# A new order of work in the engines' queues, from unit 12 of the third block to the end

## The chip, the cores and the metric

One core of one Trainium2 chip runs the whole kernel. The metric is device time in microseconds of that core, lower is better. The engines are TensorE (PE), VectorE (DVE), ScalarE (ACT), GpSimd (POOL) and SyncE (SP); each works off its own queue in the order of the program text, and DMAs are issued by SP and by ACT.

## The reference

Three layers follow each other on 1536 tokens of width 512, all in float32.

```python
# 1: attention with decay, 2 x 8 heads, 768 steps of 64, in blocks of 64
out[:, :, sl] = ((qb @ kb.T) * Dmask) @ vb + (qb * lam_pow) @ kv_state
# 2: x @ w_in (512 x 2048), leaky relu, @ w_out (2048 x 512)
g = np.maximum(0.01 * h, h)
# 3: h = x @ w_in (512 x 1024)
solu = h * softmax(h)
ln = (solu - mean(solu)) / np.sqrt(var(solu) + 1e-06) * g_ln
out = ln @ w_out            # 1024 x 512
```

## The kernel before

Every float32 matrix is split into a high and a low piece, and each product is three groups of matmuls: high by high, high by low, low by high. The pieces of an activation are made by a copy on ACT (high) and a subtraction on DVE (low).

Layer 2 runs in three blocks of 512 tokens; a block has 16 units, one for each 128 columns of the hidden layer. Unit f computes L1 (`l1_mm`, 12 matmuls into one of two `hps` banks), ACT and DVE turn the bank into a high and a low piece (`l1_split`: Prelu, copy, subtraction), and L2 of the unit before (`l2_mm`, 12 matmuls) adds to the four `acc` banks. After unit 15 the four banks are split into `xhi` and `xlo`, the input of layer 3 (`l2_split`, lines 458 to 461).

Layer 3 runs over six pairs of token tiles of 128 rows, two pairs to a block. A pair's h (two tiles by 1024) comes from seven products of six matmuls (`product`, Strassen's scheme in Winograd's form), each into a bank, and `h2_sum` adds the bank into the tiles. Product 1 is copied out of its bank by ACT (line 609); the others are added by DVE, four of them with a running maximum. In pairs 1 to 5 products 1 and 2 share bank `aps[0]`, 6 and 3 `aps[1]`, 5 and 4 `hps[0]`. The sums of x that five of the products need are made by POOL (`sums_x`) and split by ACT and DVE (`pieces_x`, lines 545 and 547).

Each of the twelve tiles t is then normed: `norm_max` (DVE), `norm_exp` (ACT), `norm_mul` (DVE: multiply, scale, and a transpose inside 32 x 32 blocks, line 646), `norm_square` (ACT, then two small POOL operations that give the row factor). `ln_turn` moves the blocks with 16 DMAs of 32 KB into a tile `lt`, so that the tile is turned; n of the 16 are issued by ACT, the rest by SP (line 663). `ln_pieces` splits the turned tile (ACT line 685, DVE line 687). `out_mm` does 24 matmuls into bank `acc[2]` or `acc[3]` (line 703), ACT evicts with the row factor (line 706), SP stores. Tiles 9 and 11 are turned by TensorE (`ln_transpose`, line 670).

The order of the text is the order of each queue; nothing reorders it. Pair 0 lies in the units 12 to 15 of the third block, two products after the L2 of units 12, 13 and 14 (`turn0`) and the last in unit 15. Both of its tiles are normed and turned in unit 15, ACT issuing 6 and 8 of the DMAs. Then come, in this order, `l2_split`, pair 1 with tile 0's pieces, output tiles 0 and 2, pair 2, and so on (lines 1027 to 1054). `h2(p, late, between, early)` puts a tile's pieces at one of three places of a pair; ACT issues 4 of the 16 DMAs of each later tile, right behind its `norm_square`.

Of the kernel before, what the change touches and what calls it, by code (L numbers as in the profile page):

```python
# [16 lines left out]
P = 128  # L17
# [12 lines left out]
FF2 = 1024  # L30
# [14 lines left out]
def fused_kernel(ctx: ExitStack, tc: tile.TileContext, att, vt, tab, cst, w_in, w_out, w_in2, w_out2, out):  # L45
# [590 lines left out]
    def norm_mul(t):  # L636

        e, h = wide(t, 0), wide(t, 1)
        dve.scalar_tensor_tensor(e, h, 1.0, e, op0=ALU.mult, op1=ALU.mult, accum_out=col(t, SU))  # L639
        dst, src = h, e  # L640
        if t not in ON_PE:
            src = e.rearrange("p (k j c) -> p j k c", j=GRP, c=32)
            dst = h.rearrange("p (j k c) -> p j k c", j=GRP, c=32)
        dve.tensor_scalar(dst, src, float(FF2), col(t, SU), op0=ALU.mult, op1=ALU.subtract)  # L644
        if t not in ON_PE:
            dve.transpose(e, h)  # L646
# [6 lines left out]
    def ln_turn(t, n_act):  # L653

        blocks = wide(t, 0)
        n = FF2 // GRP
        lt[t] = tmp.tile([P, GRP, n], F32, tag="s", name="lt")
        for far in range(GRP):
            for i in range(GRP):
                j = (i + far) % GRP  # L660
                src, dst = (slice(32 * g, 32 * g + 32) for g in (i, j))
                queue = act if far * GRP + i >= GRP * GRP - n_act else sync
                queue.dma_start(out=lt[t][dst, i], in_=blocks[src, j * n : (j + 1) * n])  # L663
        et.pop(t)
# [17 lines left out]
    def ln_pieces(t):  # L682
        lnt[t] = wp.tile([P, 2, KF2, P], F32R, tag="w", name="ln")
        for src, hi, lo in halves_of(t):
            act.copy(hi, src)  # L685
        for src, hi, lo in halves_of(t):
            dve.tensor_tensor(lo, src, hi.bitcast(F32), op=ALU.subtract)  # L687

    outs = []

    def out_mm(t):
        t_ = lnt.pop(t)
        hi, lo = t_[:, 0], t_[:, 1]
        terms = [(hi, k, s) for k in range(KF2) for s in range(2)] + [(lo, k, 0) for k in range(KF2)]
        osb = gp.tile([P, 512], F32, tag="glo", name="osb")
        parts = 2 if t == NT - 1 else 1
        n = 512 // parts
        for j in range(parts):
            po = acc[2 + len(outs) % 2]
            outs.append(t)  # L700
            cols = slice(j * n, (j + 1) * n)
            for i, (x, k, s) in enumerate(terms):
                pe.matmul(  # L703
                    po[:, 0:n], x[:, k], w2_t["b", k][:, s, cols], start=(i == 0), stop=(i == len(terms) - 1)
                )
            act.activation(osb[:, cols], po[:, 0:n], AF.Copy, scale=col(t, RS))
            load(sync, out=out[t * P : (t + 1) * P, cols], in_=osb[:, cols])
# [139 lines left out]
    def both_pieces(n):  # L847
# [15 lines left out]
        14: [lambda: join(nB[3]), lambda: both_pieces(nB[3])],  # L863
# [12 lines left out]
        13: [lambda: bits(nB[3])],  # L876
    }

    def turn0(n):

        for k, bank in {12: ((1, 0), (6, 1)), 13: ((5, 0), (2, 1)), 14: ((3, 0), (7, 1))}[n]:
            product(0, k, aps[bank])
        if n == 12:
            t = tmp.tile([P, 2, 512], F32, tag="s", name="u")
            up[0] = [t[:, 0], t[:, 1], None]
        if n == 13:
            new_tile(0)
            new_tile(2)
            up[0][2] = et[2][:, 0, 0]
        for k, bank in {12: ((1, 0), (6, 1)), 13: ((5, 0), (2, 1)), 14: ((3, 0), (7, 1))}[n]:  # L890
            h2_sum(0, k, aps[bank])
            if k == 3:
                norm_max(0)
                norm_exp(0)

    load_weights(NLEAD)
    for i, u in enumerate(items[1:], 1):
# [31 lines left out]
        elif i == len(items) - 1:  # L929
            product(0, 4, aps[0])  # L930
            act.activation(bank, bank, AF.Prelu, alpha=0.01)
            ghi = gp.tile([P, 512], F32R, tag="ghi", name="ghi")
            glo = gp.tile([P, 512], F32R, tag="glo", name="glo")
            act.copy(ghi, bank)
            norm_mul(0)
            h2_sum(0, 4, aps[0])
            norm_max(2)
            norm_exp(2)
            dve.tensor_tensor(glo, bank, ghi.bitcast(F32), op=ALU.subtract)
            gt[u] = ghi, glo  # L940
            norm_square(0)
            ln_turn(0, 6)
            norm_mul(2)
            norm_square(2)
            ln_turn(2, 8)
        elif i > 2:
# [7 lines left out]
            l1_split(u, bank)  # L954
            for do in behind.get(i - last, ()):
# [32 lines left out]
        if i - last in (12, 13, 14):  # L988
            turn0(i - last)
# [4 lines left out]
    def h2(p, late=None, between=lambda: None, early=None):  # L994
# [5 lines left out]
        banks = {1: aps[0], 6: aps[1], 5: hps[0], 7: hps[1], 2: aps[0], 3: aps[1], 4: hps[0]}  # L1000
        for n in (1, 6, 5, 7, 2, 3, 4):
            product(p, n, banks[n])
            h2_sum(p, n, banks[n])
            if n == 2 and early is not None:
                ln_pieces(early)
            if n == 3:
                norm_max(t)
                norm_exp(t)
        norm_max(t2)
        norm_exp(t2)  # L1010
        if late is not None:
            ln_pieces(late)
        norm_mul(t)
        norm_square(t)
        if t not in ON_PE:
            ln_turn(t, 4)
        between()
        norm_mul(t2)
        norm_square(t2)
        if t2 not in ON_PE:  # L1020
            ln_turn(t2, 4)

    def between1():
        ln_pieces(2)
        pieces_x(1)

    l2_split(items[-1][0])
    h2(1, early=0, between=between1)
    out_mm(0)
    out_mm(2)  # L1030
# [3 lines left out]
    h2(2, early=1, between=lambda: ln_pieces(3))  # L1034
    out_mm(1)
    h2(3, late=4)
    ln_pieces(6)
    pieces_x(2)
    out_mm(3)
    out_mm(4)  # L1040
# [78 lines left out]
```

## Time and profile before

| | us |
|---|---|
| median of 3 runs (465.14 to 466.38) | 466.3 |
| profiled execution, device time | 467.38 |
| its span, first to last instruction | 465.6 |
| PE busy in the span | 434.7 |
| DVE busy | 265.7 |
| ACT busy | 219.7 |
| POOL busy | 89.6 |

The span is read from the first to the last instruction of the core; the device time is a little longer. Busy times say how long an engine worked in all, not whether it worked when it was wanted: that is read from the waits and from the stretches. "Granted clock" is the share of TensorE's full 2.4 GHz that it was given; 0.5 is the lower level of 1.2 GHz, and a stretch between the two is a mixture.

### The profile page before, as it was taken

What the parts mean: (1) busy time and instruction counts of PE and PEld (TensorE: products, weight loads), DVE (VectorE), ACT (ScalarE), POOL (GpSimd) and SP (SyncE); (2) the same over time, 40 slices, a digit from 0 to 9 for tenths busy, and PEclk for the clock granted to TensorE, in tenths of its full rate; (3) what the DMA queues carried; (4) which work ended last, traced back from release to release, by engine and by line L of the source; (5) the groups of instructions that cost most, each with busy time, mean ns of one, the idle gap of its engine ahead of it and who ended that gap; (6) DMA issues with size and microseconds to landing.
All of it is one profiled execution on the core that took longest, in us unless ns stands there. A gap on an engine that the chain in (4) does not pass through costs nothing.

```text
span 465.6 us, 7971 instructions
## 1 busy us (share of the span) xinstructions
PE 434.7 (93%) x3224; PEld 355.4 (76%) x3224; DVE 265.7 (57%) x382; ACT 219.7 (47%) x351; POOL 89.6 (19%) x94
## 2 busy tenths in 40 slices
PE   8699999999999999999999999997789587996997
PEld 4678788888888888888888888886568475884786
DVE  4589999988231212111538887774757456655530
ACT  3488897785432222212545775354334233422531
POOL 0500111222020205400005140008529102000200
PEclk9999999999999999999999999999979979898999
DMA  8799809361130301000257004002022211212111
GB/s 293 261 336 351 316 13 327 99 239 40 57 94 0 92 1 46 0 1 1 90 180 271 1 27 155 1 10 82 6 56 75 57 58 51 85 32 63 41 69 45
DMA packets 23700, 46.86 MB, mean 101 GB/s; under 512 B 4336, under 2 KB 12016, under 8 KB 23152
## 3 DMA queue, kind: packets, MB, share of 16 engines
q1 hardware_dynamic: 21312, 44.46, 28.0%
q10 hardware_dynamic: 2352, 1.90, 1.4%
q8 instruction: 25, 0.41, 0.4%
q14 instruction: 11, 0.09, 0.1%
HBM read 37.95 MB, written 3.15 MB: 88 GB/s over the span
## 4 chain that ended last, share of the span: by engine, by line
PE 74%; DVE 11%; ACTq 3%; DMA 3%; ACT 3%; issue 3%; SPq 2%; DVEq 0%
PE hps L439 28%; PE acc L456 27%; PE aps L575 5%; PE acc L703 5%; ACTq L663 3%; DVE e L639 3%; DVE e L646 2%; SPq L663 2%; DVE ln L687 2%; DMA lt<-e 2%; DVE e L644 2%; PE hps L575 1%; PE aps L250 1%; PE aps L264 1%; DVE e L593 1%
## 5 line engine op out<-in xcount | busy, mean ns | idle before, releaser
L439 PE MATMUL hps<-xhi,wio 128*128 128x512 f32 x384 | 102.7, 390 | 0.5 <-ACT xhi L299 0.5
L456 PE MATMUL acc<-ghi,wio 128*128 128x512 f32 x384 | 96.1, 392 | 0.0
L447 DVE TENSOR_TENSOR glo<-hps,ghi 128x512 fp32r<-128x512 f32 x47 | 32.4, 689 | 99.7 <-ACT ghi L445 99.6
L439 PEld LDWEIGHTS hps<-xhi,wio 128*128 128x128 f32 x384 | 72.0, 188 | 15.5 <-ACT xhi L299 0.6
L456 PEld LDWEIGHTS acc<-ghi,wio 128*128 128x128 f32 x384 | 71.3, 188 | 15.6 <-ACT ghi L445 0.4
L703 PE MATMUL acc<-wb,ln 128*128 128x512 f32 (+1 forms) x312 | 69.3, 382 | 4.8 <-ACT ln L685 4.8
L442 ACT ACTIVATE hps<-hps 128x512 f32<-128x512 f32 x47 | 27.4, 583 | 90.3 <-PE hps L439 90.2
L703 PEld LDWEIGHTS acc<-wb,ln 128*128 128x128 f32 x312 | 56.7, 193 | 16.1 <-ACT ln L685 5.2
L456 PE MATMUL acc<-glo,wio 128*128 128x512 f32 x192 | 51.3, 389 | 0.0
L439 PE MATMUL hps<-xlo,wio 128*128 128x512 f32 x192 | 51.3, 389 | 0.0
L456 PEld LDWEIGHTS acc<-glo,wio 128*128 128x128 f32 x192 | 36.0, 188 | 7.5
L439 PEld LDWEIGHTS hps<-xlo,wio 128*128 128x128 f32 x192 | 36.0, 188 | 7.5
L165 POOL TENSOR_TENSOR qk<-qk,masks 128x512 f32<-128x512 f32 x8 | 11.9, 1487 | 140.8 <-PE hps L196 109.6
L370 DVE SCALAR_TENSOR_TENSOR raww<-x,raww 128x1024 uint32<-128x1024 uint32 (+1 forms) x28 | 32.4, 1157 | 3.8 <-ACT raww L354 2.0
L575 PE MATMUL aps<-wa,xhi 128*128 128x512 f32 x68 | 21.1, 437 | 13.0 <-ACT e L609 13.0
L379 DVE SCALAR_TENSOR_TENSOR x<-x,raww 128x1024 uint32<-128x1024 uint32 (+1 forms) x28 | 31.3, 1119 | 0.1
L350 ACT ACTIVATE x<-raww 128x1024 f32<-128x1024 f32 (+1 forms) x28 | 27.8, 992 | 5.3 <-DMA raww<-in_w_in_dram 5.3
L633 ACT ACTIVATE e<-e,small 128x1024 f32<-128x1024 f32 x12 | 13.8, 1151 | 33.1 <-DVE small L627 32.9
L445 ACT CAST ghi<-hps 128x512 fp32r<-128x512 f32 x47 | 27.6, 587 | 1.5
L354 ACT ACTIVATE raww<-raww 128x1024 uint32<-128x1024 uint16 (+1 forms) x28 | 27.7, 989 | 0.0
L575 PEld LDWEIGHTS aps<-wa,xhi 128*128 128x128 f32 x68 | 14.1, 212 | 17.1 <-ACT e L609 14.2
L687 DVE TENSOR_TENSOR ln<-lt,ln 128x1024 fp32r<-128x1024 f32 x10 | 12.5, 1249 | 24.7 <-DMA lt<-e 15.1
(139 smaller groups left out, 565.1 us busy)
## 6 DMA issues: line engine op xcount, KB each, us to landing
raww<-in_w_out_dram SPq DMA_DIRECT2D x23, 512.0 KB, 5.5
raww<-in_w_in_dram SPq DMA_DIRECT2D x16, 512.0 KB, 5.6
qk<-in_att_dram SPq DMA_DIRECT2D x8, 512.0 KB, 4.1
raww<-in_w_in_dram SPq DMA_DIRECT2D x4, 1024.0 KB, 4.7
lt<-e SPq DMA_DIRECT2D x114, 32.0 KB, 1.9
out_dram<-osb SPq DMA_DIRECT2D x11, 256.0 KB, 2.2
ldw<-in_att_dram SPq DMA_DIRECT2D x7, 384.0 KB, 5.4
kv<-in_att_dram SPq DMA_DIRECT2D x16, 128.0 KB, 3.2
```

What stands on the lines that cost most here:

```text
L350: act.activation(x, raw[:, :, 1].bitcast(F32), AF.Copy, scale=HI_SCALE)
L354: act.activation(raw[:, :, 0], raw.bitcast(U16)[:, :, 1], AF.Copy, scale=LO_SCALE)
L370: dve.scalar_tensor_tensor(raw[:, :, 0], x.bitcast(U32), 3, raw[:, :, 0], op0=ALU.logical_shift_left, op1=ALU.bitwise_or)
L379: dve.scalar_tensor_tensor(xu, xu, 0x80000000, raw[:, :, 0], op0=ALU.bitwise_and, op1=ALU.bitwise_or)
L439: pe.matmul(bank, w[:, s, k], x[b][:, k], start=(i == 0), stop=(i == len(terms) - 1))
L442: act.activation(bank, bank, AF.Prelu, alpha=0.01)
L445: act.copy(ghi, bank)
L447: dve.tensor_tensor(glo, bank, ghi.bitcast(F32), op=ALU.subtract)
L456: pe.matmul(acc[m], w[:, s, m], g, start=(f == 0 and first), stop=(f == NF - 1 and last))
L575: pe.matmul(bank, x, Bp[w, j][:, s], start=(i == 0), stop=(i == len(terms) - 1))
L663: queue.dma_start(out=lt[t][dst, i], in_=blocks[src, j * n : (j + 1) * n])
L703: pe.matmul(po[:, 0:n], x[:, k], w2_t["b", k][:, s, cols], start=(i == 0), stop=(i == len(terms) - 1))
```

## The change

It changes the order of work from unit 12 of the third block to the end. The parts:

- `turn0`: pair 0's products are spread. 1 and 6 follow the L2 in unit 12, 2 stands between L1 and L2 of unit 13, 5 and 3 behind that L2, 7 between L1 and L2 of unit 14, 4 behind that L2. Each product's sum follows it at once.
- Tile 0 is normed and turned in unit 14, tile 2 in unit 15. The last weight pieces (`nB[3]`) move from unit 14 to unit 15.
- `ln_turn` is split into `by_sync` (the first 12 DMAs, on SP) and `by_act` (the last 4, on ACT), which stand at places of their own; tile 10 has all 16 on SP. The tile `lt` is allocated in `norm_mul`.
- `ln_pieces` is split into `ln_high` (ACT) and `ln_low` (DVE).
- `out_mm` is split into the matmuls and a store that it returns, to be called later. It uses all four `acc` banks in turn.
- `l2_split` of the last block becomes four copies on ACT behind pair 1's first product, and four subtractions on DVE, one behind each of the sums 6, 5, 7 and 2.
- `h2` takes lists of what to do behind a given product; the text after it is an order written out by hand.

The diff:

```diff
--- before.py
+++ after.py
@@ -636,6 +636,8 @@
     def norm_mul(t):
 
         e, h = wide(t, 0), wide(t, 1)
+        if t not in ON_PE:
+            lt[t] = tmp.tile([P, GRP, FF2 // GRP], F32, tag="s", name="lt")
         dve.scalar_tensor_tensor(e, h, 1.0, e, op0=ALU.mult, op1=ALU.mult, accum_out=col(t, SU))
         dst, src = h, e
         if t not in ON_PE:
@@ -650,18 +652,21 @@
         pool.tensor_scalar(col(t, VA), col(t, SA), col(t, SA), col(t, SQ), op0=ALU.mult, op1=ALU.add)
         pool.tensor_tensor(col(t, RS), col(t, VA), nhalf, op=ALU.pow)
 
-    def ln_turn(t, n_act):
+    def ln_turn(t, queue, parts):
 
         blocks = wide(t, 0)
         n = FF2 // GRP
-        lt[t] = tmp.tile([P, GRP, n], F32, tag="s", name="lt")
-        for far in range(GRP):
-            for i in range(GRP):
-                j = (i + far) % GRP
-                src, dst = (slice(32 * g, 32 * g + 32) for g in (i, j))
-                queue = act if far * GRP + i >= GRP * GRP - n_act else sync
-                queue.dma_start(out=lt[t][dst, i], in_=blocks[src, j * n : (j + 1) * n])
-        et.pop(t)
+        for x in parts:
+            far, i = divmod(x, GRP)
+            j = (i + far) % GRP
+            src, dst = (slice(32 * g, 32 * g + 32) for g in (i, j))
+            queue.dma_start(out=lt[t][dst, i], in_=blocks[src, j * n : (j + 1) * n])
+
+    def by_sync(t, n=12):
+        ln_turn(t, sync, range(n))
+
+    def by_act(t, n=12):
+        ln_turn(t, act, range(n, GRP * GRP))
 
     def ln_transpose(t, banks):
         e = et.pop(t)[:, 1].rearrange("p a b -> p (a b)").rearrange("p (k c) -> p k c", k=KF2)
@@ -679,32 +684,34 @@
             (lt[t][q].rearrange("p (a b) -> p a b", a=4), *(x[:, 4 * q : 4 * q + 4] for x in (hi, lo))) for q in range(2)
         ]
 
-    def ln_pieces(t):
+    def ln_high(t):
         lnt[t] = wp.tile([P, 2, KF2, P], F32R, tag="w", name="ln")
         for src, hi, lo in halves_of(t):
             act.copy(hi, src)
+
+    def ln_low(t):
         for src, hi, lo in halves_of(t):
             dve.tensor_tensor(lo, src, hi.bitcast(F32), op=ALU.subtract)
 
-    outs = []
-
-    def out_mm(t):
-        t_ = lnt.pop(t)
-        hi, lo = t_[:, 0], t_[:, 1]
+    outs, osbs = [], {}
+
+    def out_mm(t, j=0, parts=1):
+        hi, lo = lnt[t][:, 0], lnt[t][:, 1]
         terms = [(hi, k, s) for k in range(KF2) for s in range(2)] + [(lo, k, 0) for k in range(KF2)]
-        osb = gp.tile([P, 512], F32, tag="glo", name="osb")
-        parts = 2 if t == NT - 1 else 1
+        if j == 0:
+            osbs[t] = gp.tile([P, 512], F32, tag="glo", name="osb")
         n = 512 // parts
-        for j in range(parts):
-            po = acc[2 + len(outs) % 2]
-            outs.append(t)
-            cols = slice(j * n, (j + 1) * n)
-            for i, (x, k, s) in enumerate(terms):
-                pe.matmul(
-                    po[:, 0:n], x[:, k], w2_t["b", k][:, s, cols], start=(i == 0), stop=(i == len(terms) - 1)
-                )
-            act.activation(osb[:, cols], po[:, 0:n], AF.Copy, scale=col(t, RS))
-            load(sync, out=out[t * P : (t + 1) * P, cols], in_=osb[:, cols])
+        po = acc[len(outs) % 4]
+        outs.append(t)
+        cols = slice(j * n, (j + 1) * n)
+        for i, (x, k, s) in enumerate(terms):
+            pe.matmul(po[:, 0:n], x[:, k], w2_t["b", k][:, s, cols], start=(i == 0), stop=(i == len(terms) - 1))
+        return lambda: out_store(t, po[:, 0:n], cols)
+
+    def out_store(t, po, cols):
+        osb = osbs[t]
+        act.activation(osb[:, cols], po, AF.Copy, scale=col(t, RS))
+        load(sync, out=out[t * P : (t + 1) * P, cols], in_=osb[:, cols])
 
 
 
@@ -860,7 +867,6 @@
         11: [lambda: pieces_w4(1), lambda: bits(nB[1])],
         12: [lambda: both_pieces(nB[1]), lambda: words(nB[2])],
         13: [lambda: join(nB[2]), lambda: both_pieces(nB[2]), lambda: words(nB[3])],
-        14: [lambda: join(nB[3]), lambda: both_pieces(nB[3])],
     }
     behind = {
         3: [lambda: words(nA[0])],
@@ -873,25 +879,27 @@
         10: [lambda: both_pieces(nB[0]), lambda: words(nB[1])],
         11: [lambda: join(nB[1])],
         12: [lambda: bits(nB[2])],
-        13: [lambda: bits(nB[3])],
+        14: [lambda: norm_mul(0), lambda: norm_square(0), lambda: by_sync(0), lambda: by_act(0), lambda: bits(nB[3])],
     }
 
-    def turn0(n):
-
-        for k, bank in {12: ((1, 0), (6, 1)), 13: ((5, 0), (2, 1)), 14: ((3, 0), (7, 1))}[n]:
+    def turn0(*todo):
+
+        for k, bank in todo:
             product(0, k, aps[bank])
-        if n == 12:
-            t = tmp.tile([P, 2, 512], F32, tag="s", name="u")
-            up[0] = [t[:, 0], t[:, 1], None]
-        if n == 13:
-            new_tile(0)
-            new_tile(2)
-            up[0][2] = et[2][:, 0, 0]
-        for k, bank in {12: ((1, 0), (6, 1)), 13: ((5, 0), (2, 1)), 14: ((3, 0), (7, 1))}[n]:
+            if k == 1:
+                t = tmp.tile([P, 2, 512], F32, tag="s", name="u")
+                up[0] = [t[:, 0], t[:, 1], t[:, 0]]
+            if k == 2:
+                new_tile(0)
+            if k == 7:
+                new_tile(2)
             h2_sum(0, k, aps[bank])
             if k == 3:
                 norm_max(0)
                 norm_exp(0)
+
+    between = {13: [(2, 0)], 14: [(7, 1)]}
+    after = {12: [(1, 0), (6, 1)], 13: [(5, 1), (3, 0)], 14: [(4, 0)]}
 
     load_weights(NLEAD)
     for i, u in enumerate(items[1:], 1):
@@ -927,22 +935,15 @@
             join(4, OUT)
             word_lo(5)
         elif i == len(items) - 1:
-            product(0, 4, aps[0])
-            act.activation(bank, bank, AF.Prelu, alpha=0.01)
-            ghi = gp.tile([P, 512], F32R, tag="ghi", name="ghi")
-            glo = gp.tile([P, 512], F32R, tag="glo", name="glo")
-            act.copy(ghi, bank)
-            norm_mul(0)
-            h2_sum(0, 4, aps[0])
             norm_max(2)
+            l1_split(u, bank)
             norm_exp(2)
-            dve.tensor_tensor(glo, bank, ghi.bitcast(F32), op=ALU.subtract)
-            gt[u] = ghi, glo
-            norm_square(0)
-            ln_turn(0, 6)
+            join(nB[3])
+            high(nB[3])
             norm_mul(2)
-            norm_square(2)
-            ln_turn(2, 8)
+            by_sync(2)
+            by_act(2)
+            low(nB[3])
         elif i > 2:
             part = OUT if i == 3 else None
             high(pair_at(i, 1), part)
@@ -952,6 +953,7 @@
             for do in before.get(i - last, ()):
                 do()
             l1_split(u, bank)
+            turn0(*between.get(i - last, ()))
             for do in behind.get(i - last, ()):
                 do()
             if s is not None:
@@ -985,73 +987,133 @@
         if i == last - 2:
             t, t2 = (tmp.tile([P, KD, HB], F32, tag="s", name="xf") for _ in range(2))
             sums_x(0, t, t2[:, 0:2], t2[:, 2:4])
-        if i - last in (12, 13, 14):
-            turn0(i - last)
+        turn0(*after.get(i - last, ()))
     l2_mm(items[-1])
     t = wp.tile([P, 2, KD, HB], F32, tag="w", name="xf")
     sums_x(1, t[:, 0], t[:, 1, 0:2], t[:, 1, 2:4])
 
-    def h2(p, late=None, between=lambda: None, early=None):
+    BANKS = {1: aps[0], 6: aps[1], 5: hps[0], 7: hps[1], 2: aps[0], 3: aps[1], 4: hps[0]}
+
+    def h2(p, **after):
 
         t, t2 = tiles_of(p)
         new_tile(t)
         new_tile(t2)
         up[p] = [et[t][:, 0, 0], et[t2][:, 0, 1], et[t2][:, 0, 0]]
-        banks = {1: aps[0], 6: aps[1], 5: hps[0], 7: hps[1], 2: aps[0], 3: aps[1], 4: hps[0]}
         for n in (1, 6, 5, 7, 2, 3, 4):
-            product(p, n, banks[n])
-            h2_sum(p, n, banks[n])
-            if n == 2 and early is not None:
-                ln_pieces(early)
+            product(p, n, BANKS[n])
+            h2_sum(p, n, BANKS[n])
+            for do in after.get(f"p{n}", ()):
+                do()
             if n == 3:
                 norm_max(t)
                 norm_exp(t)
+                for do in after.get("chain", ()):
+                    do()
         norm_max(t2)
         norm_exp(t2)
-        if late is not None:
-            ln_pieces(late)
-        norm_mul(t)
-        norm_square(t)
-        if t not in ON_PE:
-            ln_turn(t, 4)
-        between()
-        norm_mul(t2)
-        norm_square(t2)
-        if t2 not in ON_PE:
-            ln_turn(t2, 4)
-
-    def between1():
-        ln_pieces(2)
-        pieces_x(1)
-
-    l2_split(items[-1][0])
-    h2(1, early=0, between=between1)
-    out_mm(0)
-    out_mm(2)
+
+    def split2(m):
+        dve.tensor_tensor(xlo[-1][:, m], acc[m], xhi[-1][:, m].bitcast(F32), op=ALU.subtract)
+
+    def split2_high():
+        for m in range(KD):
+            act.copy(xhi[-1][:, m], acc[m])
+
+    h2(
+        1,
+        p1=[split2_high],
+        p6=[lambda: split2(0)],
+        p5=[lambda: split2(1)],
+        p7=[lambda: split2(2), lambda: ln_high(0), lambda: norm_square(2)],
+        p2=[lambda: split2(3)],
+        chain=[lambda: ln_low(0), lambda: ln_high(2)],
+    )
+    norm_mul(1)
+    norm_square(1)
+    by_sync(1)
+    ln_low(2)
+    pieces_x(1)
+    put0 = out_mm(0)
+    put0()
+    by_act(1)
+    norm_mul(3)
+    norm_square(3)
+    by_sync(3)
+    put2 = out_mm(2)
     t = ap1.tile([P, KD, HB], F32, tag="kv", name="xf")
     t2, t3 = (gp.tile([P, 2, HB], F32, tag="ghi", name="xf") for _ in range(2))
     sums_x(2, t, t2, t3)
-    h2(2, early=1, between=lambda: ln_pieces(3))
-    out_mm(1)
-    h2(3, late=4)
-    ln_pieces(6)
-    pieces_x(2)
-    out_mm(3)
-    out_mm(4)
-    h2(4, late=5, between=lambda: ln_pieces(7))
-    out_mm(6)
-    out_mm(5)
-    h2(5, late=8)
-    out_mm(7)
+    put2()
+    h2(2, p5=[lambda: ln_high(1), lambda: ln_low(1), lambda: by_act(3)])
+    norm_mul(4)
+    ln_high(3)
+    norm_square(4)
+    by_sync(4)
+    by_act(4)
+    ln_low(3)
+    put1 = out_mm(1)
+    put1()
+    norm_mul(6)
+    by_sync(6)
+    def late6():
+        norm_square(6)
+        by_act(6)
+    h2(3, p1=[late6], p2=[lambda: ln_high(4)])
+    ln_low(4)
+    norm_mul(5)
+    pieces_x(2, slice(0, 1))
+    norm_square(5)
+    by_sync(5)
+    by_act(5)
+    put3 = out_mm(3)
+    put3()
+    norm_mul(7)
+    pieces_x(2, slice(1, 3))
+    norm_square(7)
+    by_sync(7)
+    ln_high(6)
+    ln_low(6)
+    put4 = out_mm(4)
+    put4()
+    h2(4, p1=[lambda: by_act(7)], p5=[lambda: ln_high(5), lambda: ln_low(5)])
+    norm_mul(8)
+    ln_high(7)
+    norm_square(8)
+    by_sync(8)
+    by_act(8)
+    ln_low(7)
+    put6 = out_mm(6)
+    put6()
+    norm_mul(10)
+    norm_square(10)
+    by_sync(10, 16)
+    put5 = out_mm(5)
+    put5()
+    h2(5, p5=[lambda: ln_high(8), lambda: ln_low(8)])
+    norm_mul(9)
+    norm_square(9)
+    ln_high(10)
+    ln_low(10)
+    norm_mul(11)
+    norm_square(11)
+    put = out_mm(7)
+    put()
+    put = out_mm(8)
     ln_transpose(9, aps)
-    ln_pieces(10)
-    ln_pieces(9)
-    out_mm(8)
+    ln_high(9)
+    put()
+    ln_low(9)
+    put = out_mm(10)
     ln_transpose(11, hps)
-    ln_pieces(11)
-    out_mm(10)
-    out_mm(9)
-    out_mm(11)
+    ln_high(11)
+    put()
+    ln_low(11)
+    put = out_mm(9)
+    put()
+    for j in range(2):
+        put = out_mm(11, j, 2)
+        put()
 
 
     last_of = {}
```

## Rows read from the trace of the kernel before

**Rows 1.** The page's 40 slices: granted TensorE clock in tenths.

```profile
PEclk9999999999999999999999999999979979898999
```

**Rows 2.** Windows, units 12 to 15: busy time (instructions) of each engine, clock, DMA.

```profile
287.97:316.53 28.56, 28.56 (x127) 23.66 (x126) 21.97 (x35) 12.97 (x21) 2.60 (x4) 1.00 0.05 13
```

**Rows 3.** Waits of PE behind 287: engine, line, releaser: us, times, longest.

```profile
PE aps L575 <- ACT e L609: 13.0, 3, 6.0
PE acc L703 <- ACT ln L685: 4.8, 1, 4.8
PE aps L575 <- ACT sa L545: 3.3, 1, 3.3
PE aps L670 <- DVE e L644: 1.0, 1, 1.0
```

**Rows 4.** Timeline of PE behind 316: start, us, line, operands, count [idle before].

```profile
324.94 1.19 PE L575 MATMUL aps<-wa,xhi 128*128 128x512 f32 x4 [2.81 <-ACT e L609]
...
339.56 7.82 PE L703 MATMUL acc<-wb,ln 128*128 128x512 f32 x24 [4.80 <-ACT ln L685]
347.22 1.07 PE L575 MATMUL aps<-wa,xhi 128*128 128x512 f32 x4
...
356.74 5.60 PE L703 MATMUL acc<-wb,ln 128*128 128x512 f32 x24
362.18 1.07 PE L575 MATMUL aps<-wa,xhi 128*128 128x512 f32 x4
...
373.76 2.07 PE L575 MATMUL aps<-wa,xhi 128*128 128x512 f32 x4 [5.98 <-ACT e L609]
...
378.63 1.07 PE L575 MATMUL hps<-wa,xhi 128*128 128x512 f32 x4
...
438.36 1.09 PE L670 MATMUL aps<-fix,e 128*128 128x128 f32 x8 [1.01 <-DVE e L644]
...
445.59 16.89 PE L703 MATMUL acc<-wb,ln 128*128 128x512 f32 x96
```

**Rows 5.** Timeline of ACT and its DMA issues (ACTq), around 312 and 372.

```profile
312.60 1.15 ACT L633 ACTIVATE e<-e,small 128x1024 f32<-128x1024 f32 x1 [1.47 <-DVE small L627]
312.61 1.34 ACTq L663 DMA_DIRECT2D lt<-e  x2
...
369.98 2.44 ACTq L663 DMA_DIRECT2D lt<-e  x4
372.55 0.69 ACT L706 ACTIVATE osb<-acc,small 128x512 f32<-128x512 f32 x1 [2.63 <-DMA lt<-e]
373.13 0.58 ACT L609 COPY e<-aps 128x512 f32<-128x512 f32 x1
```

**Rows 6.** Groups of instructions behind 316.5: busy us, mean ns of one, idle before.

```profile
L639 DVE SCALAR_TENSOR_TENSOR e<-e 128x1024 f32<-128x1024 f32 x10 | 12.3, 1233 | 0.9 <-ACT e L633 0.9
...
L633 ACT ACTIVATE e<-e,small 128x1024 f32<-128x1024 f32 x10 | 11.5, 1150 | 29.8 <-DVE small L627 29.6
L646 DVE STREAM_TRANSPOSE e<-e 128x1024 f32<-128x1024 f32 x9 | 11.2, 1246 | 0.3
...
L685 ACT CAST ln<-lt 128x1024 fp32r<-128x1024 f32 x10 | 10.5, 1050 | 10.6 <-DMA lt<-e 10.6
...
L644 DVE TENSOR_SCALAR e<-e,small 128x1024 f32<-128x1024 f32 x10 | 7.5, 753 | 0.4
```

**Rows 7.** DMA issues of the page: count, KB each, median us to landing.

```profile
lt<-e SPq DMA_DIRECT2D x114, 32.0 KB, 1.9
```

**Rows 8.** Timeline of SP's issues, tiles 1 and 3: start, us, count.

```profile
335.94 8.96 SPq L663 DMA_DIRECT2D lt<-e  x12
...
346.39 7.79 SPq L663 DMA_DIRECT2D lt<-e  x12
```

**Rows 9.** Timeline of DVE in unit 13: the subtraction of l1_split.

```profile
297.69 0.69 DVE L447 TENSOR_TENSOR glo<-hps,ghi 128x512 fp32r<-128x512 f32 x1 [2.33 <-ACT ghi L445]
```

## The prediction

> **What bounds the kernel now.** I read the 40 slices of the page first: the granted clock is at 9 or more tenths until the last third and dips there [rows 1]. Then the windows by stage: in units 12 to 15 TensorE is busy for 28.56 of 28.56 us at clock 1.00 [rows 2]. Nothing can be won there; what can be won lies behind the end of that stretch, 316.53, where the first product of pair 1 starts.
>
> Third, TensorE's waits: 13.0 us on the ACT copy of line 609 (three times), 4.8 on the high piece of a turned tile, 3.3 on a high piece of the x sums, 1.0 on the norm in front of the last transposes: 22.1 in all [rows 3].
>
> Fourth, TensorE in order of time, for the price of work without waits. An output tile of 24 matmuls takes 362.18 - 356.74 = 5.44, a product of six a quarter of it, 1.36; the last 96 matmuls (two whole tiles, two halves) take 16.89; a set of eight transposes 1.09 with its drain, which I take as 0.85 [rows 4]. Behind 316.53 stand 35 products, 9 output tiles, two sets of transposes and the last group: 47.6 + 49.0 + 1.7 + 16.9 = 115.2. The last matmul ends at 445.59 + 16.89 = 462.48, so 145.95 pass: 30.8 more than the work. Of these 22.1 are the waits and 8.7 follow them, above all as a lower clock. Behind the 5.98 us wait four matmuls take 2.07 where they take 1.07 at the 2.4 GHz level, so TensorE came out of that wait at 1.2 GHz; the two products there take 378.63 - 373.76 = 4.87 in place of 2.72, and the output tile behind the 4.8 us wait 347.22 - 339.56 = 7.66 in place of 5.44 [rows 4].
>
> Fifth, what ACT does ahead of the longest wait: four DMA issues (2.44), then an output's eviction, then the copy of line 609 that frees the bank [rows 5]. The product in the bank was long done; ACT's order was the wait. The steps between two tiles, on DVE and ACT, are 0.75 to 1.25 each [rows 6], short against the 20.4 us that a pair costs TensorE (7 x 1.36 + 2 x 5.44).
>
> **The change part by part.** The matmuls and the operations of DVE and ACT are the same in number. Of the 160 transfers of turned tiles SP issued 114 [rows 7], ACT 46; now it is 124 and 36. The rest is order. I put the new order on each engine's queue and add durations [rows 4 to 9], each operation starting when its queue and its inputs are there; sums and evictions of 512 columns count as 0.6 each, as the subtraction of 0.69 does to its successor [rows 9].
>
> *Units 12 to 15.* The seven products of pair 0 stay ahead of 316.53, two of them now between an L1 and an L2. Product 3 writes the bank that sum 2 reads, and sum 2 stands behind the subtraction of unit 13, which starts at 297.69 [rows 9]: sum 2 runs 298.3 to 299.0, product 3 could start at 298.85. Wait: 0.2. A gain is excluded, since TensorE has no idle time here [rows 2]; above, the bound is 2.81, the shortest wait on a bank [rows 4]. I take 0.2, from the row of the subtraction itself.
>
> TensorE then goes on: product 3 to 300.4, L1 to 303.1, product 7 to 304.5, L2 to 307.2, product 4 to 308.55, L1 of unit 15 to 311.3, L2 twice to 314.0 and 316.7. Tile 0's exp is done at 303.0 and its norm follows product 7's sums on DVE: 306.4 + 1.25 + 0.75 + 1.25 = 309.65. ACT issues its four transfers to 312.1, ahead of unit 15's Prelu, whose matmuls end at 311.3; Prelu and copy end at 313.4, and the L2 of that unit asks at 314.0. Covered by 0.6; with no cover it costs at most those 2.44.
>
> *Tile 2.* Exp from 313.4 to 314.7; DVE joins a weight to 315.2, multiplies, scales and transposes to 318.45. ACT issues to 321.0, then copies product 1 out of its bank by 321.6; TensorE asks for the bank after four products, at 322.15. This is the wait of 2.81 of before, when 14 issues and four copies of `xhi` stood ahead of that copy; now cover is 0.5. The copies of `xhi` run behind it to 323.7, and the subtractions, spread over DVE's sums, let sum 3 end at 327.9.
>
> *Output tiles 0 and 2.* SP's issues for tile 0 run to 317.6 and land by 319.5; its high piece is ready at 324.9, its low one at 329.3. TensorE comes to it at 326.2 and, 16 matmuls (3.6) later, to the low one at 329.8. Tile 2: SP 318.5 to 326.4, landed 328.3; high piece 330.6, asked for at 331.65; low piece 334.7, asked for at 335.3. So the 4.8 us wait goes, with covers of 1.1 and 0.5.
>
> *Pairs 2 to 5.* x sums of block 1: all pieces by 337.0, asked for from 338.5 on. Bank copies: pair 2 at 341.4 against 342.55, pair 3 at 356.2 against 357.5, pair 4 at 375.3 against 378.0, pair 5 at 394.4 against 398.3. High pieces: tile 1 at 344.4 against 346.6, tile 4 at 363.4 against 367.05, tile 10 at 409.9 against 414.2, the others earlier by more. x sums of block 2: 368.3 and 373.0 against 373.85 and 375.2. The last transposes wait for nothing. Here twelve SP issues count 7.9 [rows 8] and landing 1.9 [rows 7].
>
> *Waits added.* ACT now waits for the landing of tiles 1, 5 and 8 in the middle of pairs 2, 4 and 5; behind each stand exp and the next pieces. No row shows this order. Bounds: nothing (landed before ACT's turn; there is no gain beyond the work itself) to 5.98, the longest wait on ACT, with 2.15 of clock behind it. I take nothing, by the covers above, and keep 8.1 for the range. SP's stores of outputs stand among the turns at one issue each, their evictions done by then.
>
> **The sum.** 316.53 + 115.2 + 0.2 = 431.9; with 0.3 for the places where cover is 0.5 to 0.6, 432.2. Last eviction and store stay: 465.6 - 462.48 = 3.1, span 435.3. The profiled execution took 467.38 for its 465.6, so 437.1; the median of the runs, 466.3, lies 1.1 under it: 436.0.
>
> **Rivals.** *1. A stall stays where ACT waits.* ACT's sequencer runs ahead of its engine (issues from 312.61 beside an exp begun at 312.60 [rows 5]), but not past a wait. If a turned tile lands later than I add, the next bank copy is late: one such stall costs 2.8 to 6.0, with clock up to 8.1: 439 to 444, two about 449. For: covers of 0.5 at three places. Against: only the first two tiles' covers are that thin. Chance 0.27.
>
> The Trainium skill, TensorE: Matmul & The Clock Gate, section "Architectural detail: the array is 16× 32×32, not 1× 128×128", calls ScalarE's queue a strict FIFO. This trace agrees: the issues at 312.61 run ahead of the engine, nothing overtakes on it.
>
> *2. SP is the pace.* From 309.7 it has 124 issues and six stores to tile 10's landing, at p each; then 1.9 to land, 18.7 for its piece, two output tiles, transposes and the last halves, 3.1 to the end and 0.7 from the span to the median: 334.1 + 130 p. At 7.79 / 12 = 0.65 that is 419, under the forecast; at 8.96 / 12 = 0.75, the slowest series, 432 [rows 8]. It decides from 0.79: at 0.85 445, at 0.95 458. Against: SP issued 24 per pair before as well. Chance 0.05.
>
> *3. Slower: the same queue past 1.02 us an issue,* where 334.1 + 130 p passes 466.3; at 1.2 it is 490. For: SP's tiles now follow each other almost without gaps, with stores between. Against: no series comes near. Chance 0.02.
>
> *4. Issuing is not what holds ACT.* Then the three waits on line 609 stay, 13.0, with some 4 of clock behind two of them: 453. Against: the eviction at 372.55 follows the issues at once [rows 5]. Chance 0.03.
>
> The Trainium skill, DMA: Bandwidth & Descriptors, section "Issuing engines are not separate DMA queues", says that starting DMAs on several engines saves only the sequencer's time, usually small beside the transfer. By it the moved issues would save next to nothing, which is rival 4; the trace differs, with four issues at 2.44 against 1.9 to landing.
>
> *5. Nothing changes:* the waits come back under other names, 465 to 467. Chance 0.01; no single wait of that size is in sight.
>
> **How the numbers follow.** Forecast 0.62 (434.5 to 438.5), rivals 0.27, 0.05, 0.02, 0.03, 0.01. With no wait at all the sum is 435.5, and the lowest run lies 1.2 under the median: low end 434.3. Up, the range takes in one full stall: 444. Some 0.13 is left out. A measurement of this kernel tells 0.3% (1.4 us) from no change. Faster 0.96, same 0.02, slower 0.02.
>
> **What would show it.** Right: TensorE busy without a wait above 1 us from 316 to 432 at clock 1.0; its waits on lines 609 and 685 gone; pair 1's first product still at 316.5 to 317. Wrong: a TensorE wait on ACT with ACT's own wait on a landing just ahead of it (rival 1), SP issuing back to back up to tile 10 (2 and 3), or a slice behind 316 with a clock under 0.8.

## The result and the profile after

The new order takes 436.7 us in the median of four runs (436.3 to 437.2); the old one 466.3 on the same chip (465.1 to 467.4). The ratio is 0.9365, with a 95% interval of 0.934 to 0.939. On another chip the two were run again: 436.3 and 465.4, ratio 0.9368 (0.9345 to 0.9392). Forecast were 436.0 and a range of 434.3 to 444.0.

| profiled execution | before | after |
|---|---|---|
| device time | 467.38 | 437.16 |
| span | 465.6 | 435.3 |
| first matmul of L1 | 25.64 | 23.07 |
| first product of pair 1 | 316.53 | 314.31 |
| end of the last matmul | 462.48 | 432.22 |
| from the first L1 to the last matmul | 436.84 | 409.15 |

The last line is the measure that I use below: the stretch ahead of the first L1 is the same code in every kernel, and its length differs from one execution to the next. Two executions of the kernel after gave 409.15 and 409.71 (e10 below), so a difference of some 0.6 says nothing.

The page's clock line and the waits of TensorE behind 280 (engine, line, releaser: us, times, longest) in the kernel after:

```profile
PEclk9999999999999999999999999999999999999999
```

```profile
PE aps L575 <- ACT e L609: 1.9, 2, 1.6
```

The dips of [rows 1] are gone, and of the 22.1 us of [rows 3] 1.9 are left. TensorE in order of time (start, us, line, operands, count, idle before), to be laid beside [rows 4]:

```profile
23.07 2.11 PE L439 MATMUL hps<-xhi,wio 128*128 128x512 f32 x8 [0.47 <-ACT xhi L299]
...
294.91 1.52 PE L575 MATMUL aps<-wa,sb 128*128 128x512 f32 x6
296.49 1.66 PE L575 MATMUL aps<-wa,sa 128*128 128x512 f32 x6
297.99 1.07 PE L439 MATMUL hps<-xhi,wio 128*128 128x512 f32 x4
...
314.31 1.07 PE L575 MATMUL aps<-wa,xhi 128*128 128x512 f32 x4
...
320.18 1.19 PE L575 MATMUL aps<-wa,xhi 128*128 128x512 f32 x4 [0.27 <-ACT e L609]
...
324.41 11.28 PE L708 MATMUL acc<-wb,ln 128*128 128x512 f32 x48
...
357.73 1.20 PE L575 MATMUL aps<-wa,xhi 128*128 128x512 f32 x4 [1.65 <-ACT e L609]
...
420.77 11.45 PE L708 MATMUL acc<-wb,ln 128*128 128x512 f32 x72
```

Output tiles 0 and 2 now run as one block of 48 matmuls, where 4.8 us stood between them and the second ran in part at the lower clock (7.66 in place of 5.44 [rows 4]). The same line of the kernel before, for the start:

```profile
25.64 1.65 PE L439 MATMUL hps<-xhi,wio 128*128 128x512 f32 x6 [0.47 <-ACT xhi L299]
```

The one wait of size is at pair 3's bank, 1.65 us. DVE and POOL ahead of it, and ACT (start, us, line, operands):

```profile
342.51 2.20 DVE L694 TENSOR_TENSOR ln<-lt,ln 128x1024 fp32r<-128x1024 f32 x1 [1.16 <-DMA lt<-e]
...
347.30 0.68 DVE L593 CUSTOM_DVE_ANT_0 e<-hps,e 128x512 f32<-128x512 f32 x1
...
348.76 2.19 DVE L641 SCALAR_TENSOR_TENSOR e<-e 128x1024 f32<-128x1024 f32 x1 [0.52 <-ACT e L633]
...
351.00 1.65 DVE L646 TENSOR_SCALAR e<-e,small 128x1024 f32<-128x1024 f32 x1
352.68 1.25 DVE L648 STREAM_TRANSPOSE e<-e 128x1024 f32<-128x1024 f32 x1
```

```profile
342.33 1.29 POOL L514 TENSOR_TENSOR xf<-xhi,xlo 128x512 f32<-128x512 f32 x1
...
347.19 1.30 POOL L517 TENSOR_TENSOR xf<-xf 128x512 f32<-128x512 f32 x1
348.57 1.29 POOL L518 TENSOR_TENSOR xf<-xf 128x512 f32<-128x512 f32 x1
349.95 2.15 POOL L519 TENSOR_TENSOR xf<-xf 128x512 f32<-128x512 f32 x1
```

```profile
353.96 2.45 ACTq L663 DMA_DIRECT2D lt<-e  x4
356.52 0.69 ACT L713 ACTIVATE osb<-acc,small 128x512 f32<-128x512 f32 x1 [2.68 <-POOL small L652]
357.10 0.58 ACT L609 COPY e<-aps 128x512 f32<-128x512 f32 x1
```

Tile 4's multiply takes 2.19 and its scale 1.65 while POOL adds the x sums; the means before were 1.23 and 0.75 [rows 6]. Ahead of them in DVE's queue the low piece of tile 1 (line 694) takes 2.20, also beside a sum of POOL; at 326.86 in the same trace one takes 1.23. So the transpose ends some 2.8 later, ACT's four issues wait for it, and eviction and bank copy stand behind the issues (the eviction's row names POOL, but it starts as the issues end): the order of [rows 5] once more, in small.

### The profile page after: what moved, and what is told of

It reads as the page before. It is cut to its first block, busy times and chain, and to the rows that moved or that the text cites. A ratio compares the mean times of both kernels' runs of the same rounds, so it can differ in the third digit from the quotient of the medians.

```text
span 435.3 us, 7979 instructions
## 1 busy us (share of the span) xinstructions
PE 426.6 (98%) x3224; PEld 350.2 (80%) x3224; DVE 269.6 (62%) x382; ACT 219.8 (50%) x351; POOL 102.5 (24%) x94
## 3 DMA queue, kind: packets, MB, share of 16 engines
q10 hardware_dynamic: 1872, 1.58, 1.3%
## 4 chain that ended last, share of the span: by engine, by line
PE 64%; DVE 13%; ACT 6%; SPq 3%; issue 3%; ACTq 0%; DMA 0%; DVEq 0%
PE hps L439 21%; PE acc L456 21%; PE acc L708 11%; PE aps L575 4%; SPq L663 3%; PE hps L575 2%; DVE x L379 2%; DVE e L641 2%; PE aps L250 2%; DVE raww L370 1%; DVE x L360 1%; DVE e L646 1%; PE aps L264 1%; DVE glo L447 1%; ACT raww L354 1%
## 5 line engine op out<-in xcount | busy, mean ns | idle before, releaser
L708 PE MATMUL acc<-wb,ln 128*128 128x512 f32 (+1 forms) x312 | 67.2, 374 | 0.0
L708 PEld LDWEIGHTS acc<-wb,ln 128*128 128x128 f32 x312 | 55.2, 188 | 10.5 <-DVE ln L694 0.4
L634 POOL TENSOR_SCALAR small<-small 128x1 f32<-128x1 f32 x12 | 8.2, 680 | 65.3 <-ACT e L633 64.9
L409 ACT CAST wio<-x 128x1024 fp32r<-128x1024 f32 (+1 forms) x21 | 17.7, 845 | 11.1 <-DVE x L379 11.1
```

Source lines behind the costliest of these rows:

```text
L409: act.copy(t[:, 0, halves], x[:, halves])
L708: pe.matmul(po[:, 0:n], x[:, k], w2_t["b", k][:, s, cols], start=(i == 0), stop=(i == len(terms) - 1))
```

## The experiments

Each time is the median of its runs; the ratio is to runs of the kernel before on the same chip; the stretch is the one from the first L1 to the last matmul, in one profiled execution.

| kernel | median | ratio to before (95%) | stretch |
|---|---|---|---|
| e1, old order, all by SP | 445.1 | 0.9554 to 0.9595 | 417.6 |
| e2, old order, square and ACT's transfers of tiles 6, 10 later | 452.7 | 0.9713 to 0.9757 | 425.8 |
| e3, new, tile 6 early | 442.1 | 0.9493 to 0.9533 | 414.7 |
| e4, new, x sums late | 434.7 | 0.9331 to 0.9364 | 407.2 |
| e5, new, old units 12 to 15 | 435.0 | 0.9298 to 0.9379 | 407.9 |
| e6, new, split first | 437.9 | 0.9354 to 0.9435 | 410.5 |
| e7, new, all by SP | 446.3 | 0.9538 to 0.9649 | 418.4 |
| e8, new, x sums early | 441.0 | 0.9422 to 0.9508 | 413.6 |
| e9, e4 and e5, tile 2 by 10 and 6 | 433.4 | 0.9285 to 0.9336 | 406.1 |
| e10, the new kernel again | 436.3 | 0.9345 to 0.9392 | 409.7 |
| e11, new, ACT's transfers at once | 443.8 | 0.9502 to 0.9560 | 417.5 |

My theory: what ACT does ahead of a bank copy or a piece makes the waits, the DMA issues in its queue above all. Rival: issuing does not hold ACT; transfers, DVE or SP's pace do.

**e1.** The old kernel with no transfer issued by ACT (for `ln_turn(2, 8)` and `ln_turn(t2, 4)` alike):

```diff
-            ln_turn(0, 6)
+            ln_turn(0, 0)
...
-            ln_turn(t, 4)
+            ln_turn(t, 0)
```

> The old order, but SP issues all 160 transfers of turned tiles and ACT none. If the time that ACT spends issuing stands in front of the bank copies, each wait of TensorE on ACT loses about the 2.44 us of four issues (the first, behind 14 issues, goes whole), with some clock: 466.3 to about 454 (451 to 458), and the waits that stay (3.5 and 1.7 in front of pairs 3 and 5) show ACT's norm_square behind DVE in front of the copy. If issuing does not hold ACT, and transfers or DVE set the waits: 465 to 467, or later by SP's longer series. If issuing were the whole cause: 438 to 442.

Measured: 445.1, far under what I expected. TensorE's waits in it:

```profile
PE acc L703 <- ACT ln L685: 3.0, 1, 3.0
PE aps L575 <- ACT e L609: 2.2, 2, 1.4
PE aps L575 <- ACT sa L545: 1.6, 1, 1.6
PE aps L670 <- DVE e L644: 1.2, 1, 1.2
PE aps L575 <- DVE sa L547: 0.3, 1, 0.3
```

Taking the issues from ACT alone saves 19.2 us of stretch, where the whole change saves 27.7, and the rival falls. Why the wait in front of pair 3 went to 0.85 and not to 3.5 is seen on ACT, from the square of tile 4 to the bank copy, with [rows 5] beside it:

```profile
352.22 1.06 ACT L649 ACTIVATE masks<-e 128x1024 bf16<-128x1024 f32 x1 [1.12 <-DVE e L644]
353.19 0.19 ACT L649 ACTIVATION_READ_ACCUMULATOR masks<-e 128x1 f32 x1
353.28 1.03 ACT L685 CAST ln<-lt 128x1024 fp32r<-128x1024 f32 x1
357.60 1.06 ACT L649 ACTIVATE masks<-e 128x1024 bf16<-128x1024 f32 x1 [3.29 <-DVE e L644]
358.56 0.19 ACT L649 ACTIVATION_READ_ACCUMULATOR masks<-e 128x1 f32 x1
358.65 0.67 ACT L706 ACTIVATE osb<-acc,small 128x512 f32<-128x512 f32 x1
359.22 0.57 ACT L609 COPY e<-aps 128x512 f32<-128x512 f32 x1
```

```profile
360.52 1.06 ACT L649 ACTIVATE masks<-e 128x1024 bf16<-128x1024 f32 x1 [1.11 <-DVE e L644]
361.49 0.19 ACT L649 ACTIVATION_READ_ACCUMULATOR masks<-e 128x1 f32 x1
361.80 2.46 ACTq L663 DMA_DIRECT2D lt<-e  x4
364.43 1.05 ACT L685 CAST ln<-lt 128x1024 fp32r<-128x1024 f32 x1 [2.76 <-DMA lt<-e]
```

The second fence is the kernel before. Two series of issues stood in that one chain: tile 4's kept back the piece of tile 3, for which DVE waited before it could norm tile 6, whose square, issues and the copy followed. From the start of the square to that of the copy it is 7.0 here and 12.6 there. I had counted one.

**e2.** The old order; `norm_square` and ACT's four transfers of tiles 6 and 10 (`later`) go behind sum 1 of the next pair:

```diff
         norm_mul(t2)
+        if t2 in (6, 10):
+            ln_turn(t2, 4, range(12))
+            return
...
-    h2(3, late=4)
+    h2(3, late=4, first=lambda: later(6))
```

> The old order with one edit: norm_square and ACT's four transfers of tiles 6 and 10 move behind sum 1 of the next pair. If the order on ACT in front of the bank copy is the cause, the waits of 5.98 and 4.17 us go with the clock behind them (2.15 and about 1.7): about 452 (450 to 456), though the wait on the x sums of block 2 may grow. If the copy is late for another reason (DVE, the product itself): 465 to 467.

Measured: 452.7, as the theory had it; place alone is worth 11.1 of stretch here (436.8 - 425.8). The copies in front of pairs 3 and 5 are no longer waited for; 1.96 stay at pair 3, on a sum of DVE, and the wait on the x sums grows from 3.28 to 4.14.

**e3.** The same edit undone in the new kernel, for tile 6:

```diff
+    norm_square(6)
     by_sync(6)
-    def late6():
-        norm_square(6)
-        by_act(6)
-    h2(3, p1=[late6], p2=[lambda: ln_high(4)])
+    by_act(6)
+    h2(3, p2=[lambda: ln_high(4)])
```

> The new order with one edit undone: norm_square and ACT's four transfers of tile 6 stand ahead of pair 3 again. If the place of these on ACT decides, the bank copy of pair 3 ends near 361.5 instead of 357.7, TensorE's wait there grows from 1.65 to about 5.3 and the clock falls behind it: 436.7 to 442.5 (441 to 444.5). If the cover elsewhere takes it up: 436.5 to 437.5.

Measured: 442.1, with TensorE's row at pair 3, and the issues in front of the copy on ACT:

```profile
360.65 2.07 PE L575 MATMUL aps<-wa,xhi 128*128 128x512 f32 x4 [5.37 <-ACT e L609]
```

```profile
357.42 2.55 ACTq L663 DMA_DIRECT2D lt<-e  x4
360.01 0.59 ACT L609 COPY e<-aps 128x512 f32<-128x512 f32 x1 [2.63 <-DMA lt<-e]
```

A wait of 5.37, and four matmuls at 2.07, the 1.2 GHz level, behind it: one placement on ACT, of four issues and a square, costs 5.5 us of stretch.

**e11.** All four late parts of ACT put back:

```diff
     by_sync(1)
+    by_act(1)
...
     put0()
-    by_act(1)
```

and so for tiles 3, 6 (as in e3) and 7.

> The new order with ACT's four transfers of tiles 1, 3, 6 and 7 put back right behind SP's twelve (6 with its norm_square, as in e3). If the place of these issues in ACT's queue is the cause, waits of about 1, 1.6, 5.4 and 1.2 come at x sums 1 and the bank copies of pairs 2, 3 and 4, with some 2.5 of clock: 446 (443 to 449). If only tile 6 matters: 442.1, as e3.

Measured: 443.8; TensorE waits 4.40 at pair 2 and 2.22 at pair 3, not at pair 4:

```profile
344.92 2.08 PE L575 MATMUL aps<-wa,xhi 128*128 128x512 f32 x4 [4.40 <-ACT e L609]
...
363.91 1.19 PE L575 MATMUL aps<-wa,xhi 128*128 128x512 f32 x4 [2.22 <-ACT e L609]
```

```profile
335.20 2.43 DVE L547 TENSOR_TENSOR xlo<-xf,xhi 128x1024 fp32r<-128x1024 f32 x3 [2.54 <-ACT xhi L545]
```

At pair 2 two series stand in one chain again: tile 1's four issues keep back the x pieces, DVE waits 2.54 for these before it norms tile 3, and tile 3's own issues stand ahead of the bank copy. The single prices don't add up; that the wait at pair 2 gives pair 3 time that it lacked is how I read it, and no run isolates it. In the new order the place of these issues, with tile 6's square, is worth 8.4 (417.5 - 409.2), and in the old one their presence 19.2. With the four places undone, 19.3 of the 27.7 still stay (436.8 - 417.5). That rests on the rest of the new order: eight issues in place of fourteen ahead of pair 1, pieces that stand ahead of the next tile's issues, tile 10 wholly on SP, the outputs' four banks and later stores. Only parts of it are undone by themselves below (e5, e6); its division stays open.

**e7.** The other end: no issue on ACT in the new order.

```diff
-    def by_sync(t, n=12):
+    def by_sync(t, n=16):
...
-    def by_act(t, n=12):
+    def by_act(t, n=16):
```

> The new order with all 16 transfers of every tile on SP. If ACT's issue time is what costs, the wait of 1.65 goes: 435.1. If SP then is the pace (16 issues at 0.64 take 10.3, 21.6 a pair with two stores, against 20.4 of TensorE), tile 10 lands at about 416 to 418, some 3 to 4 after TensorE asks: 439 (437.5 to 441), the wait in front of the last output tiles.

Measured: 446.3, outside what either theory expected. SP is the pace, as rival 2 had it, but TensorE pays at another place: its longest wait is 5.32 at pair 5's bank, not for tile 10 (three others are 1.1 to 1.3). TensorE's row, then ACT's and SP's:

```profile
405.82 2.08 PE L575 MATMUL aps<-wa,xhi 128*128 128x512 f32 x4 [5.32 <-ACT e L609]
```

```profile
399.24 1.05 ACT L690 CAST ln<-lt 128x1024 fp32r<-128x1024 f32 x1 [4.04 <-PE hps L575]
...
405.20 0.57 ACT L609 COPY e<-aps 128x512 f32<-128x512 f32 x1
```

```profile
386.87 10.86 SPq L663 DMA_DIRECT2D lt<-e  x16
```

SP issues tile 7 until 397.73, and ACT's piece of tile 7 starts 1.5 later, about when the last transfer can have landed (1.8 from issue to landing, the median; the row names TensorE, whose last product ahead of this piece in the text ended at 384.2). Square, evictions and the bank copy stand behind it: a late transfer becomes a late copy, which is rival 1. The new order with all by SP (418.4) is no better than the old one with all by SP (417.6). That the new order is 9.2 better with 36 issues left on ACT is the work of the split: these stand where ACT has time, and SP has room again.

**e4.** POOL's x sums of block 2 go behind tile 4's square:

```diff
     put2 = out_mm(2)
...
-    sums_x(2, t, t2, t3)
     put2()
...
     norm_square(4)
...
+    sums_x(2, t, t2, t3)
```

> The new order with POOL's x sums of block 2 moved behind norm_square of tile 4. If those sums slowed DVE's multiply (2.19 for 1.23) and scale (1.65 for 0.75) of tile 4, both fall back, the 1.65 us wait of TensorE falls under 0.5: 436.7 to about 435.3 (434.8 to 435.8). If the slow DVE rows have another cause: 436.7 (436.2 to 437.2), rows still slow.

Measured: 434.7, at the low edge of the expected range; tile 4's rows of DVE and the low piece of tile 1 fall back, and the wait at pair 3 is gone.

```profile
341.72 1.23 DVE L694 TENSOR_TENSOR ln<-lt,ln 128x1024 fp32r<-128x1024 f32 x1 [1.14 <-DMA lt<-e]
...
347.00 1.23 DVE L641 SCALAR_TENSOR_TENSOR e<-e 128x1024 f32<-128x1024 f32 x1 [0.51 <-ACT e L633]
...
348.27 0.75 DVE L646 TENSOR_SCALAR e<-e,small 128x1024 f32<-128x1024 f32 x1
```

Counted from pair 2's first product, tile 4's transpose ends 2.9 earlier than in the kernel after (350.30 - 334.76 against 353.93 - 335.52).

**e8.** The same sums the other way:

```diff
+    sums_x(2, t, t2, t3)
     norm_mul(1)
...
     put2 = out_mm(2)
...
-    sums_x(2, t, t2, t3)
     put2()
```

> The new order with POOL's x sums of block 2 moved the other way, ahead of norm_mul of tile 1. If the sums slow DVE's operations on two SBUF tensors and its scale, norm, low piece and x pieces between pairs 1 and 2 stretch by about 1 us each (1.2 to 2.2, 0.75 to 1.65), waits of 1.7 to 2.7 come there and the 1.65 at pair 3 goes: 437.7 (436.9 to 439.5). If POOL does not touch DVE: 435.1, DVE's rows as before.

Measured: 441.0, above the expected range. DVE between pairs 1 and 2, and TensorE's row at pair 2:

```profile
333.08 5.70 DVE L547 TENSOR_TENSOR xlo<-xf,xhi 128x1024 fp32r<-128x1024 f32 x3
338.70 2.31 DVE L641 SCALAR_TENSOR_TENSOR e<-e 128x1024 f32<-128x1024 f32 x1
...
341.05 1.63 DVE L646 TENSOR_SCALAR e<-e,small 128x1024 f32<-128x1024 f32 x1
```

```profile
345.03 1.31 PE L575 MATMUL aps<-wa,xhi 128*128 128x512 f32 x4 [4.08 <-ACT e L609]
```

The three x pieces take 5.70, 2.42 in the kernel after. I had given them 1 us more; it is 3.3.

**e6.** `l2_split` whole ahead of pair 1, as it was.

```diff
+    l2_split(items[-1][0])
     h2(
         1,
-        p1=[split2_high],
-        p6=[lambda: split2(0)],
-        p5=[lambda: split2(1)],
-        p7=[lambda: split2(2), lambda: ln_high(0), lambda: norm_square(2)],
-        p2=[lambda: split2(3)],
+        p7=[lambda: ln_high(0), lambda: norm_square(2)],
```

> The new order with the split of the last block whole ahead of pair 1. The copy of product 1 then stands behind four copies of xhi (2.06 us): TensorE's wait of 0.27 there grows to about 2.3: 438.7 (438.0 to 439.5). If the cover takes it up: 436.7.

Measured: 437.9, just under the expected range. The wait at pair 1 grows to 2.22, as expected; the stretch by only 1.35, and pair 3's wait of 1.65 does not come any more.

**e5.** Units 12 to 15 in the old order, but with 12 transfers by SP and 4 by ACT for each tile; the rest new (cut):

```diff
-    between = {13: [(2, 0)], 14: [(7, 1)]}
-    after = {12: [(1, 0), (6, 1)], 13: [(5, 1), (3, 0)], 14: [(4, 0)]}
+        for k, bank in {12: ((1, 0), (6, 1)), 13: ((5, 0), (2, 1)), 14: ((3, 0), (7, 1))}[n]:
...
+            norm_square(0)
+            by_sync(0)
+            by_act(0)
             norm_mul(2)
             by_sync(2)
             by_act(2)
```

> The new order with units 12 to 15 as they were (pair 0's products, tiles 0 and 2 normed in unit 15), but with 12 transfers by SP and 4 by ACT for each tile. If only ACT's issues in front of pair 1 mattered there, the spread of pair 0 is worth nothing: tile 0's transpose ends some 2 us later, tile 2's some 2 earlier, SP ends tile 2 at the same time: 436.4 (435.5 to 437.3). If the early norm of tile 0 is needed, waits on the bank copy and the pieces of pair 1 come back: 439 to 441.

Measured: 435.0, just under the expected range. What the change does in units 12 to 15 apart from that split, the spread of pair 0 and the early norm of tile 0, is worth nothing; without it the stretch is 1.2 shorter. One wait is left in it, of 1.14, on tile 2's high piece.

**e9.** e4 and e5 together, and tile 2's transfers split otherwise:

```diff
-            by_sync(2)
-            by_act(2)
+            by_sync(2, 10)
+            by_act(2, 10)
```

> Units 12 to 15 in the old order as in e5, POOL's sums late as in e4, and tile 2 with 10 transfers by SP and 6 by ACT. In e5 TensorE waits once, 1.14 us, on tile 2's high piece, which ACT makes late. If tile 2's landing makes it late, two transfers less on SP (1.3 us) take that wait away: from the first L1 to the last matmul 406.7, median about 434.0. If the piece waits for its buffer, freed by the output matmuls of tile 0 (the row of ACT names them), the wait stays: 407.9, about 435.0.

Measured: 433.4, the fastest here and a little under what was expected, with no wait of TensorE from 280 to the end; its stretch of 406.1 is what the prediction's work adds up to: 431.7 (316.53 + 115.2) less 25.64 (from pair 1's first product to the last matmul pass 428.82 - 313.60 = 115.22). Whether the wait of e5 went by the earlier landing or because another buffer was free stays open: two things were changed at once. e10, the new kernel beside it:

> The new kernel itself, on the same chip as the other two: 436.7 (436.0 to 437.3), from the first L1 to the last matmul 409.2.

Measured: 436.3, stretch 409.7.

## Why the prediction was right

*What bounds the kernel.* Right. Work without waits behind pair 1's start was counted as 115.2 with a place for each wait; e9 runs it at that price.

*Units 12 to 15.* The place was right, product 3 behind sum 2, the price about (0.2 forecast, 0.36 measured): product 3 starts 0.22 late (296.49 against 294.91 + 1.36) and takes 1.50, so that the stretch from unit 13's L1 to pair 1 is 26.20 against 25.84. What I did not ask is whether the part brings anything. It doesn't (e5).

*Tile 2 and the bank of pair 1.* Forecast with 0.5 of cover, measured with a wait of 0.27: tile 2's scale took 1.66 beside POOL's sums and moved the transpose.

*Output tiles 0 and 2, pairs 2, 4 and 5, the last transposes.* Covered, as forecast; no wait there.

*Pair 3.* This is the step that was mis-sized. Forecast: copy done at 356.2, asked for at 357.5, a cover of 1.3. Measured, with 2.57 (25.64 - 23.07) added so that both count from the first L1: copy done at 360.25, asked for at 358.65. TensorE came 1.15 later than forecast and the copy 4.05, so the cover became a wait of 1.65. The prediction took each of DVE's steps between two tiles at 0.75 to 1.25 [rows 6]. Beside POOL's sums the low piece, the multiply and the scale took 2.20, 2.19 and 1.65, which is 2.8 more in one chain. In that sum I left POOL's neighbourhood out, and no rival named it; e4 and e8 show it in both directions. By the prediction's own sign, no wait above 1 us, this one place failed.

*Waits added.* No cost, as taken: no row of the kernel after shows TensorE waiting for a landing. One landing does stand in pair 3's chain: ACT waits 1.60 for tile 1, until 341.42, and DVE 1.16, until 342.51. In e4 they wait 1.58 and 1.14 there, and TensorE does not wait. The cover hangs on the split between the queues: with SP's share at 16 the stretch is 9.2 longer (e7).

*The sum.* The stretch was forecast as 432.2 - 25.64 = 406.6 and measured as 409.15: 30.3 of gain forecast, 27.7 found. The missing 2.6 are the two waits (1.9 against 0.3 in the sum for thin covers), 0.2 more in units 12 to 15, some 0.3 at each wait beside the idle time itself, and 0.2 in the block of output tiles 0 and 2. At pair 3, for example, its seven products pass from 350.48 to 361.97, 11.49, of which 9.52 are work and 1.65 the wait. That the median came within 0.7 nonetheless is partly luck: the profiled execution of before reached its first L1 at 25.64, those of the kernel after and of the eleven experiments at 22.2 to 23.1, and I had taken off only 1.1 between profile and median for it. The span came out at the forecast 435.3 because a start 2.6 earlier hid a stretch 2.6 longer.

*Rivals.* Rival 1's late bank copy is what is left of the waits, at 1.9 in place of 2.8 to 8.1, but by e4 what made it late was DVE beside POOL and not a landing. Rivals 2 and 3: SP has room at 12 a tile and none at 16. Rival 4 is refuted by e1: taking the issues from ACT saved 19.2. The Trainium skill, DMA: Bandwidth & Descriptors, section "Issuing engines are not separate DMA queues", calls the time to initiate a DMA usually small beside the transfer. This case differs: one issue takes 0.61 (2.44 for four [rows 5]), against 1.9 from issue to landing [rows 7].

## What to carry to other kernels

Four DMA issues, 2.4 us together, on an engine that also frees banks cost their time once for every chain in which they stand; follow the chain through the other engines before counting them once. Move them behind the operation that the bound engine waits for, or onto a queue with room, and count that queue's issues against the period first. Durations from a trace hold for the neighbours that the operation had there: where an edit puts it beside another engine's work, look for a row with that neighbour.

## What the runs showed of the hardware

DVE and POOL exclude each other on some operations. In the kernel after, POOL's sum of line 518 runs from 348.57 to 349.86. DVE's multiply, begun at 348.76, ends at 350.95: its own 1.23 counted back from there begin at 349.72, about when the sum is done. POOL's next sum, begun at 349.95, ends at 352.10: its 1.29 counted back begin at 350.81, about when the multiply is done. DVE's scale, begun at 351.00, ends at 352.65, and its 0.75 begin at 351.90. The two take turns. The low piece shows it too: begun at 342.51 beside the sum of line 514, which ends at 343.62, it ends at 344.71, and its 1.23 begin at 343.48. DVE's transpose (1.25, as at 315.78 beside the sums of lines 513 and 514) and its sums out of a bank (0.68, as at 347.30) are as long beside POOL as without it.

The Trainium skill, SBUF — State Buffer, section "Who interferes with whom", says that DVE shares one pair of ports with GpSimd, that operations with two SBUF inputs or in a two-port mode need it, and that it is locked for the whole instruction. The rows agree with the lock: turns, not a common slowdown. The multiply and the low piece have two SBUF inputs; the transpose and the sums out of a bank have one and are untouched. The scale has one tensor as input too and took its turn; that it ran in a two-port mode would fit, but no run shows its mode.
